# Softmax-attention backward: dK/dV bursts split in odd groups, the turns moved to the fourth unit, turned dQ from group 3 to group 6, and one tile taken from GpSimd

## The chip, the cores and the metric

The kernel runs on one core of one Trainium2 chip. The metric is the time of one execution on the device in microseconds; lower is better. The kernel before has a median of 2526.64 us over 3 runs (2521.6 to 2527.84).

## The reference, cut to what matters

The computation is one block of a transformer (adaptive layer norm, multi-head attention, a squared-ReLU MLP) and its whole backward pass: 2048 positions, model width 512, 32 heads of width 16. The part that the change touches is the backward pass of the attention. The forward part of it in the reference is

```python
    q, k, v = (qkv[0], qkv[1], qkv[2])
    scale = Dh ** (-0.5)
    scores = jnp.einsum('bhqd,bhkd->bhqk', q, k) * scale
    p = _softmax(scores, axis=-1)
    o = jnp.einsum('bhqk,bhkd->bhqd', p, v)
```

and the gradients come from `jax.vjp` of the whole block. For every head the backward pass needs P = exp(scores), dP = dO V^T, dS = P * (dP - row term), and then dV = P^T dO, dK = dS^T Q and dQ = dS K. P is a 2048 x 2048 matrix for each of 32 heads, and it is computed anew.

## The kernel before, in words

The backward attention is written out by hand in `attn_bwd` (L1429 on); its instructions stand on each engine in the order of the code. It takes 32 heads in 16 **pairs** of heads: `g` counts eight quads, `jp` the two pairs of a quad (L1549, L1550). Within a pair, `c` counts four blocks of 512 keys (L1566), and `ib` sixteen tiles of 128 queries, taken in four **groups** of four (L1568, L1575). The text numbers the groups of a pair 0 to 15 (`m` in the code, L1569): groups 0 to 3 are block c = 0, and so on. Each group has four **units**, `i` = 0 to 3; "the fourth unit" is `i == 3`. A unit has two heads, a = 0 and a = 1.

What a unit does, in the order of TensorE (PE):

- For each head, `st` (L1584) computes 128 x 512 scores in a PSUM tile, and ScalarE (ACT) takes the exponential into `pu` (L1587). Right behind each `st` stands `dp` (L1509), which is dP of the unit *before*; VectorE (DVE) multiplies it with that unit's `pu` into `ds` (L1513). `st` and `dp` use opposite halves of the rows of the array. There are three PSUM buffers named "st" and three named "dp". So PE can put an `st` only when ACT has read the one three tiles earlier, and a `dp` only when DVE has read the one three earlier; as PE is in order, whatever stands behind waits too.
- After units 1 and 3, `kv_two` (L1494) adds two earlier units to dK and dV: eight matmuls into `acckv` (L1455), four of which run side by side in four groups of columns. After the last unit of a block, ACT copies `acckv` into `kvT` (L1458); the next block's first `kv` starts `acckv` anew.
- After units 0 and 2, sixteen small matmuls add to dQ in `accq` (L1478). They read `dsT`, the transposed `ds` of a group three groups earlier. The transposition is one DMA per group from the SP queue (L1530). In even groups a part of it, the first 128 x 512 tile, is done by PE and ACT instead (`turn_ds`, L1535: four transposes into an "st" buffer, L1543, and the copy L1544).
- In odd groups (`off`, L1515) one of the eight `ds` tiles, that of `i == 1` and a = 1, is not DVE's: ACT copies `dp` to SBUF (L1521; the buffers are called junk and csq by turns) and GpSimd (POOL) multiplies (L1522).
- The **turns**: dK and dV of the pair before lie transposed in `kvT`. `turn` (L1460) transposes one half of them with eight matmuls into an "st" buffer (L1468), and ACT copies it out with two copies (L1472). dQ is turned by `turn_q` (L1486): DVE scales `accq` into `dqT` (L1483), then four transposes (L1491) and one ACT copy (L1492). The turns wait in the list `turnq`; one is taken at `i == 1` of a group (L1578).

So in every pair but the first, group 1 and group 2 have a dK/dV turn at their second unit, and group 3 the turned dQ, all of the pair before. POOL issues the loads of the next quad, spread over the groups (L1570 to L1573), a small copy (`tick`) ahead of each.

Of the kernel before, what the change touches and what calls it, by code (L numbers as in the profile page):

```python
# [105 lines left out]
class K:  # L106
# [1322 lines left out]
    def attn_bwd(self):  # L1429
# [8 lines left out]
        S, D, H, NQ, ST, SC = self.S, self.D, self.H, self.NQ, self.ST, self.SC  # L1438
        G = 4
# [7 lines left out]
        pend, pendq, turnq = [], [], []  # L1447

        def kv(u):
            (T, g, jp, c, ib, kvT, pu, ds) = u  # L1450
            for j, (n, src) in enumerate((("Q", ds), ("dO", pu))):
                for a in range(2):
                    r = 64 * j + 32 * a
                    col = (2 * jp + a) * DH
                    nc.tensor.matmul(acckv[r:r + DH, :], lhsT=T[n][:, ib, col:col + DH], rhs=src[:, a, :],  # L1455
                                     start=(ib == 0), stop=(ib == ST - 1))
            if ib == ST - 1:
                nc.scalar.activation(kvT[:, 512 * c:512 * (c + 1)], acckv[:], ACT.Copy, scale=kvs[:])  # L1458

        def turn(g, jp, kvT, s0):  # L1460

            if kvT is None:
                return turn_q(g, jp)
            h0 = 4 * g + 2 * jp
            n = ST // 2
            tp = stp.tile([P, n, P], BF16, name="st")
            for st in range(n):
                nc.tensor.transpose(tp[:, st, :], kvT[:, (s0 + st) * P:(s0 + st + 1) * P], self.ident[:])  # L1468
            v = tp[:].rearrange("p s (t a e) -> p t s a e", t=2, a=2)
            for t, dst in enumerate((self.dk_t, self.dv_t)):  # L1470
                d = dst[:, s0:s0 + n, h0 * DH:(h0 + 2) * DH].rearrange("p s (a d) -> p s a d", a=2)
                nc.scalar.copy(d, v[:, t, :, :, 0:DH])  # L1472
# [19 lines left out]
            nc.scalar.copy(self.dq_t[:, :, h0 * DH:(h0 + 2) * DH], tp[:].rearrange("p b (i e) -> p (b i) e", i=G))  # L1492

        def kv_two(n=2):  # L1494
            for u in pend[2 - n:2]:
                kv(u)
            (T, g, jp, c, ib, kvT, pu, ds) = pend[1]
            del pend[:2]
            if c % 2 and ib == ST - 1 and (g, jp) == (NQ - 1, 1):
                turnq.append((g, jp, kvT, 4 * (c - 1)))  # L1500
            elif c == SC - 1 and ib == ST - 1:
                turnq.extend((g, jp, kvT, s0) for s0 in (0, ST // 2))

        def dP(u, a):

            (T, g, jp, c, ib, kvT, pu, dsg, i, grp) = u
            rd = slice(64 - 64 * jp, 128 - 64 * jp)
            dp = dpp.tile([P, 512], F32, name="dp")
            nc.tensor.matmul(dp[:], lhsT=T["dOT"][rd, ib * P:(ib + 1) * P],  # L1509
                             rhs=masked["VT"][a][rd, 512 * c:512 * (c + 1)], start=True, stop=True)  # L1510
            if a == 1 and i == 1 and off(c, ib):
                return dp
            nc.vector.tensor_tensor(dsg[:, i, a], dp[:], pu[:, a, :], ALU.mult)  # L1513

        def off(c, ib):  # L1515
            return (c * SC + ib // G) % 2 == 1

        def dP_pool(u, dp):
            (T, g, jp, c, ib, kvT, pu, dsg, i, grp) = u
            f = (self.junk6, self.csq)[(c * SC + ib // G) // 2 % 2]  # L1520
            nc.scalar.copy(f[:], dp[:])  # L1521
            nc.gpsimd.tensor_tensor(dsg[:, i, 1], f[:], pu[:, 1, :], ALU.mult)  # L1522
# [12 lines left out]
        def turn_ds(dsg, grp, skip):  # L1535

            dsT = dtp.tile([P, 8 * G, P], BF16, name="dsT")
            grp.extend((dsT, 0 if skip else 4))
            if skip:
                return  # L1540
            tp = stp.tile([P, 4, P], BF16, name="st")
            for b in range(4):
                nc.tensor.transpose(tp[:, b, :], dsg[:, 0, 0, b * P:(b + 1) * P], self.ident[:])  # L1543
            nc.scalar.copy(dsT[:, 0:4, :], tp[:])  # L1544

        tick = self.tick
        T = self.T0
        last = None
        for g in range(NQ):  # L1549
            for jp in range(2):  # L1550
                if jp == 0:
                    if g + 1 < NQ:
                        Tn, later = self.load_group(g + 1)
                    else:
                        Tn, later = None, self.wq_pieces(1) + self.load_wmt()
                    cut = len(later) // 2 if Tn else len(later)
                    pieces = self.pair_pieces(g, 1) + later[:cut]
                    later = later[cut:]
                elif g + 1 < NQ:
                    pieces = self.pair_pieces(g + 1, 0) + later  # L1560
                else:
                    pieces = [(self.xhat1_6[:, st, :], self.xhat1_d.rearrange("(st p) d -> p st d", p=P)[:, st, :])
                              for st in range(ST)]
                kvT = kvp.tile([P, S], BF16, name="kvT")
                total = len(pieces)
                for c in range(SC):  # L1566
                    c0 = 512 * c
                    for ib0 in range(0, ST, G):  # L1568
                        m = c * (ST // G) + ib0 // G  # L1569
                        while pieces and (total - len(pieces)) * SC * ST <= m * G * total:  # L1570
                            if last:
                                nc.gpsimd.tensor_copy(tick[:], last[7][0:1, 0, 0, 0:1])
                            nc.gpsimd.dma_start(*pieces.pop(0))  # L1573
                        dsg, grp = self.dsp.tile([P, G, 2, 512], BF16, name="ds"), []
                        for i in range(G):  # L1575
                            ib = ib0 + i
                            q = slice(ib * P, (ib + 1) * P)
                            if turnq and i == 1:  # L1578
                                turn(*turnq.pop(0))
                            pu = self.pup.tile([P, 2, 512], BF16, name="pu")  # L1580
                            for a in range(2):
                                stt = stp.tile([P, 512], F32, name="st")
                                rs = slice(64 * jp, 64 * jp + 64)
                                nc.tensor.matmul(stt[:], lhsT=T["QT"][rs, q], rhs=masked["KT"][a][rs, c0:c0 + 512],  # L1584
                                                 start=True, stop=True)
                                held = dP(last, a) if last else None
                                nc.scalar.activation(pu[:, a, :], stt[:], ACT.Exp, scale=self.scale)  # L1587
                                if held is not None:
                                    dP_pool(last, held)
                            if last:  # L1590
                                dS(last)
                            last = (T, g, jp, c, ib, kvT, pu, dsg, i, grp)
                            if i % 2 == 1 and len(pend) >= 4:
                                kv_two()
                            elif i % 2 == 0 and len(pendq) > 4 * G:
                                for _ in range(8 if len(pendq) > 6 * G else 4):
                                    dq(pendq.pop(0))
                            if i == 2:
                                turn_ds(dsg, grp, off(c, ib))
            T = Tn  # L1600
        with tc.manual_schedule(engines=ALL):
            for t in (2, 0):
                for p in self.wq_pieces(t):
                    nc.gpsimd.dma_start(*p)
            for a in range(2):
                dP(last, a)
            dS(last)
            while len(pend) > 2:
                kv_two()
            kv(pend[0])  # L1610
            for _ in range(2 * G):
                dq(pendq.pop(0))
            kv_two(1)
            k0, v0, k1 = [dpp.tile([P, 512], F32, name="dp") for _ in range(3)]
            self.dw_mm(k0, 1, 0, 0, ST // 2)
            turn(*turnq.pop(0))
            for _ in range(2 * G):
                dq(pendq.pop(0))
            self.dw_mm(v0, 2, 0, 0, ST // 2)
            self.dw_mm(k0, 1, 0, ST // 2, ST)  # L1620
            self.col_sum(1)
            self.dw_mm(v0, 2, 0, ST // 2, ST)
            self.col_sum(2)
            self.cs_bc(1)
            while pendq:
                dq(pendq.pop(0))
            self.cs_bc(2)
            turn(*turnq.pop(0))
            self.dw_mm(k1, 1, 1, 0, ST)
# [312 lines left out]
```

## Time and profile before

| what | value |
|---|---|
| median of 3 runs | 2526.64 us |
| the profiled execution | 2524.31 us, span 2522.4 us |
| mean granted TensorE clock | 0.998 |
| busy over the span | PE 96%, ACT 91%, DVE 68%, POOL 28% |
| backward attention, first `pu` to last | 1169.6 to 2400.5 us of the span |
| a pair without late DMAs | about 76.2 us |

The page gives busy time of each engine and the idle time ahead of each group of instructions. Two cautions for reading it. Instructions overlap: a `pu` takes 0.64 us from start to end, but the next can start 0.48 us after it, so "busy" near 100% does not say that no time is lost; the spacing of starts does. And PE's busy time counts a matmul from its start to its modelled end, and hides waits of some 0.2 us.

### The profile page before, as it was taken

To read this page: it belongs to the slowest core of one execution; us is meant where nothing else is said; L and a number is where in the kernel's file an instruction comes from. 1 tells how busy PE (TensorE), PEld (TensorE's weight loads), DVE (VectorE), ACT (ScalarE), POOL (GpSimd) and SP (SyncE) were. 2 spreads that over 40 slices of the span, in tenths; PEclk is the share of its full clock that TensorE was granted. 3 is DMA by queue.
4 is the path that set the end of the run, shared out by engine and by line. 5 is a ranking of instruction groups with operands and counts; after the bars stand their busy time and mean duration, and the time that the engine had idled before them with its cause. 6 is when DMAs were issued, how large, how long until landed. Compare 5 with 4: busy or idle time off the path is not lost.

```text
span 2522.4 us, 76903 instructions
## 1 busy us (share of the span) xinstructions
PE 2433.1 (96%) x30791; PEld 1107.9 (44%) x30791; DVE 1705.4 (68%) x3519; ACT 2296.2 (91%) x3773; POOL 713.9 (28%) x1289
## 2 busy tenths in 40 slices
PE   8999999999999999989999999999999999999998
PEld 4555555555555554673333333333333333333343
DVE  6222223422332343667999999999999999999957
ACT  7999999999999997535999999999999999999945
POOL 2344531321131022255222222222222222222223
PEclk9999999999999999999999999999999999999999
DMA  4589761441343044699999999999999999999997
GB/s 167 134 178 202 179 114 64 116 99 44 103 118 74 24 137 129 139 191 214 234 221 218 218 226 220 223 227 218 219 218 223 225 221 221 222 228 226 237 211 198
DMA packets 1260558, 446.30 MB, mean 177 GB/s; under 512 B 1204052, under 2 KB 1228246, under 8 KB 1260198
## 3 DMA queue, kind: packets, MB, share of 16 engines
q1 hardware_dynamic: 1219654, 336.29, 70.7%
q0 software_dynamic: 38464, 104.04, 13.9%
q8 instruction: 241, 3.95, 0.7%
q10 hardware_dynamic: 2080, 1.05, 0.1%
q14 instruction: 119, 0.97, 0.1%
HBM read 75.83 MB, written 64.49 MB: 56 GB/s over the span
## 4 chain that ended last, share of the span: by engine, by line
PE 59%; ACT 22%; DMA 11%; issue 4%; DVE 3%; SPq 1%; POOL 0%; DVEq 0%; ACTq 0%; POOLq 0%
ACT pu L391 18%; PE st L1584 17%; DMA dsT<-ds 8%; PE acckv L1455 8%; PE st L388 8%; PE accq L1478 5%; PE accbank L322 3%; PE dp L1509 3%; ACT pu L1587 2%; PE dps L1050 2%; PE pps L1237 2%; PE dps L995 1%; DVE ds L1513 1%; PE st L1543 1%; PE pps L631 1%
## 5 line engine op out<-in xcount | busy, mean ns | idle before, releaser
L1513 DVE TENSOR_TENSOR ds<-dp,pu 128x512 bf16<-128x512 f32 x1920 | 1178.3, 681 | 44.5 <-PE dp L1509 26.4
L1587 ACT ACTIVATE pu<-st 128x512 bf16<-128x512 f32 x2048 | 1073.9, 641 | 39.4 <-PE st L1584 21.3
L391 ACT ACTIVATE pu<-st 128x1024 bf16<-128x1024 f32 x992 | 912.2, 1077 | 5.4 <-PE st L388 5.1
L388 PE MATMUL st<-QTm,KTq 128*128 128x512 bf16 x1984 | 588.4, 377 | 19.7 <-ACT pu L391 6.1
L322 PEld LDWEIGHTS <-pu 128*128 128x128 bf16 x8192 | 347.2, 96 | 236.2 <-issue 3.2
L322 PE MATMUL accbank<-Vaug,pu 128*128 128x17 bf16 x8192 | 357.6, 171 | 1.2 <-ACT Vaug L522 0.9
L1509 PE MATMUL dp<-kvm,q 64*128 64x512 bf16 x1024 | 356.4, 382 | 2.2 <-DVE g2w L1056 0.7
L1509 PE MATMUL dp<-kvm,dOTg 64*128 64x512 bf16 x1024 | 356.2, 382 | 0.9
L1584 PE MATMUL st<-kvm,QTg 64*128 64x512 bf16 x1024 | 327.2, 381 | 10.5 <-ACT pu L1587 7.4
L1584 PE MATMUL st<-kvm,q 64*128 64x512 bf16 x1024 | 326.6, 380 | 10.8 <-ACT pu L1587 7.6
L388 PEld LDWEIGHTS <-KTq 128*128 128x128 bf16 x1984 | 188.2, 96 | 177.5 <-issue 125.9
L1522 POOL TENSOR_TENSOR ds<-junk,pu 128x512 bf16<-128x512 f32 x64 | 73.7, 1151 | 378.6 <-DVE ds L1513 336.7
L1522 POOL TENSOR_TENSOR ds<-csq,pu 128x512 bf16<-128x512 f32 x64 | 73.8, 1154 | 356.6 <-ACT csq L1521 356.6
L302 POOL DMA_DIRECT2D QTm<-QTq_d x124 | 63.5, 514 | 342.7 <-PE st L388 321.3
L1455 PE MATMUL acckv<-ds,Qg 128*16 128x512 bf16 x1024 | 154.3, 381 | 0.0
L1455 PE MATMUL acckv<-pu,dOg 128*16 128x512 bf16 x1024 | 154.2, 381 | 0.0
L1455 PE MATMUL acckv<-pu,q 128*16 128x512 bf16 x1024 | 154.0, 381 | 0.0
L1455 PE MATMUL acckv<-ds,q 128*16 128x512 bf16 x1024 | 154.0, 381 | 0.0
L329 DVE RECIPROCAL rl<-accbank 128x4 f32<-128x4 f32 x128 | 22.9, 179 | 159.5 <-PE accbank L322 159.2
L1584 PEld LDWEIGHTS <-q 64*128 64x128 bf16 x1024 | 58.1, 94 | 137.9 <-issue 104.5
L1584 PEld LDWEIGHTS <-QTg 64*128 64x128 bf16 x1024 | 57.7, 94 | 137.7 <-issue 102.7
L1509 PEld LDWEIGHTS <-q 64*128 64x128 bf16 x1024 | 88.4, 93 | 64.2 <-issue 47.4
(387 smaller groups left out, 3138.6 us busy)
## 6 DMA issues: line engine op xcount, KB each, us to landing
KTq<-KTq_d POOLq DMA_DIRECT2D x24, 512.0 KB, 3.8
duT_d<-auT POOLq DMA_DIRECT2D x3, 1792.0 KB, 8.2
aT_d<-rT POOLq DMA_DIRECT2D x3, 1792.0 KB, 11.6
KTq_d<-KTq SPq DMA_DIRECT2D x32, 128.0 KB, 2.0
QTq_d<-ev_fm SPq DMA_DIRECT2D x32, 128.0 KB, 3.4
ktm_d<-ev_tm POOLq DMA_DIRECT2D x32, 128.0 KB, 2.5
VTq_d<-vT POOLq DMA_DIRECT2D x4, 1024.0 KB, 5.8
dsT<-ds SPq DMA_TRANSPOSE x256, 7.1
```

Of the source, the lines that this page charges most:

```text
L302: nc.gpsimd.dma_start(QTm[j][32 * j:32 * j + 32, :], self.QTq_d[g, 32 * j:32 * j + 32, 512 * qc:512 * (qc + 1)])
L322: nc.tensor.matmul(acc[:, a, sub, :], lhsT=pu[:, a, sub * P:(sub + 1) * P], rhs=Vaug[:, kb, h, :], start=(kb == 0 and a == 0 and sub == 0) ...
L388: nc.tensor.matmul(stt[:, a, :], lhsT=KT[:, kb * P:(kb + 1) * P], rhs=QTm[2 * jp + a][:], start=True, stop=True)
L391: nc.scalar.activation(pu[:], stt[:], ACT.Exp, scale=self.scale)
L1050: nc.tensor.matmul(pt[:], lhsT=a[st], rhs=g_tm[:, st, :], start=(st == 0), stop=(st == ST - 1))
L1455: nc.tensor.matmul(acckv[r:r + DH, :], lhsT=T[n][:, ib, col:col + DH], rhs=src[:, a, :], start=(ib == 0), stop=(ib == ST - 1))
L1478: nc.tensor.matmul(accq[32 * i:32 * i + 32, ib0 // G, :], lhsT=T["K"][:, 4 * c + sub, col:col + 32], rhs=dsT[:, (i * 2 + a) * 4 + sub, :], ...
L1509: nc.tensor.matmul(dp[:], lhsT=T["dOT"][rd, ib * P:(ib + 1) * P], rhs=masked["VT"][a][rd, 512 * c:512 * (c + 1)], start=True, stop=True)
L1513: nc.vector.tensor_tensor(dsg[:, i, a], dp[:], pu[:, a, :], ALU.mult)
L1522: nc.gpsimd.tensor_tensor(dsg[:, i, 1], f[:], pu[:, 1, :], ALU.mult)
L1584: nc.tensor.matmul(stt[:], lhsT=T["QT"][rs, q], rhs=masked["KT"][a][rs, c0:c0 + 512], start=True, stop=True)
L1587: nc.scalar.activation(pu[:, a, :], stt[:], ACT.Exp, scale=self.scale)
```

## The change

Four edits, all in `attn_bwd`.

1. `kv_two(n)` now takes n units from the head of the list. In odd groups it is called with 1, twice: once in the middle of units 1 and 3, between the two heads, and once after them. So the burst of eight matmuls becomes two of four, with an `st` and a `dp` between them. Even groups keep bursts of eight.
2. Turns are taken at `i == 3` and no longer at `i == 1`: in groups 1 and 2 for dK/dV.
3. The turned dQ waits until group 6 (`m >= 6`).
4. In group 1 (`(c, ib // G) == (0, 1)`) the eighth `ds` tile is DVE's too; the copy by ACT and the multiplication by POOL are left out. That is 16 tiles of 128 that POOL had.

```diff
         def kv_two(n=2):
-            for u in pend[2 - n:2]:
+            for _ in range(n):
+                u = pend.pop(0)
                 kv(u)
-            (T, g, jp, c, ib, kvT, pu, ds) = pend[1]
-            del pend[:2]
-            if c % 2 and ib == ST - 1 and (g, jp) == (NQ - 1, 1):
-                turnq.append((g, jp, kvT, 4 * (c - 1)))
-            elif c == SC - 1 and ib == ST - 1:
-                turnq.extend((g, jp, kvT, s0) for s0 in (0, ST // 2))
+                (T, g, jp, c, ib, kvT, pu, ds) = u
+                if ib < ST - 1:
+                    continue
+                if c % 2 and (g, jp) == (NQ - 1, 1):
+                    turnq.append((g, jp, kvT, 4 * (c - 1)))
+                elif c == SC - 1:
+                    turnq.extend((g, jp, kvT, s0) for s0 in (0, ST // 2))
...
-            if a == 1 and i == 1 and off(c, ib):
+            if a == 1 and i == 1 and off(c, ib) and (c, ib // G) != (0, 1):
                 return dp
...
-                            if turnq and i == 1:
+                            if turnq and i == 3 and (turnq[0][2] is not None or m >= 6):
                                 turn(*turnq.pop(0))
...
                                 if held is not None:
                                     dP_pool(last, held)
+                                if a == 0 and i % 2 == 1 and off(c, ib) and len(pend) >= 4:
+                                    kv_two(1)
...
                             if i % 2 == 1 and len(pend) >= 4:
-                                kv_two()
+                                kv_two(1 if off(c, ib) else 2)
...
             while len(pend) > 2:
                 kv_two()
-            kv(pend[0])
+            kv_two(1)
```

The order of PE in an odd group is before `st dp st dp, 16 dQ, st dp st dp, 8 kv`, twice; after, `st dp st dp, 16 dQ, st dp, 4 kv, st dp, 4 kv`, twice. The number of matmuls and of DMAs is the same.

## The prediction

> **What bounds the kernel now.** I read the page's busy shares first, then busy time by stretch, then the timelines of single engines in one pair. The change touches only the backward attention, 1169.6 to 2400.5 us of the span. I take the seventh pair (1630.5 to 1706.7), in which no DMA is late, in its four blocks of four groups:
>
> ```profile
> 1630.73:1651.23 20.50, 20.10 (x294) 7.48 (x296) 19.25 (x32) 20.08 (x43) 4.87 (x11) 1.00 1.03 195
> 1651.23:1669.78 18.55, 18.18 (x268) 6.27 (x263) 18.27 (x31) 18.42 (x38) 4.93 (x11) 1.00 1.14 226
> 1669.78:1688.36 18.58, 18.21 (x268) 6.32 (x271) 18.31 (x31) 18.45 (x38) 4.93 (x11) 1.00 1.19 230
> 1688.36:1706.91 18.55, 18.21 (x263) 6.29 (x263) 18.17 (x30) 18.41 (x38) 5.03 (x11) 1.00 1.16 229
> ```
>
> The columns after the length are busy us of PE, weight loads, DVE, ACT, POOL, then clock, DMA share, GB/s. PE, DVE and ACT are all nearly full, and the first block is 1.95 us longer than the others: it holds the turns. The clock is 1.00, so the throttle plays no part. Where time is lost inside "busy" shows in ACT's and DVE's own timelines of the first block:
>
> ```profile
> 1635.31 0.73 ACT L1458 ACTIVATE kvT<-acckv,kvs 128x512 bf16<-128x512 f32 x1
> 1636.83 0.45 ACT L1472 COPY dk_t<-st 128x256 bf16<-128x256 bf16 x1
> 1639.32 0.69 ACT L1521 COPY junk<-dp 128x512 f32<-128x512 f32 x1
> ...
> 1647.20 0.58 ACT L1492 COPY dq_t<-st 128x512 bf16<-128x512 bf16 x1 [0.26 <-PE st L1491]
> ```
> ```profile
> 1631.42 5.48 DVE L1513 TENSOR_TENSOR ds<-dp,pu 128x512 bf16<-128x512 f32 x9
> 1637.54 4.60 DVE L1513 TENSOR_TENSOR ds<-dp,pu 128x512 bf16<-128x512 f32 x7 [0.63 <-PE dp L1509]
> 1642.40 2.48 DVE L1513 TENSOR_TENSOR ds<-dp,pu 128x512 bf16<-128x512 f32 x4 [0.26 <-PE dp L1509]
> 1644.80 0.68 DVE L1483 TENSOR_SCALAR dqT<-accq 128x512 bf16<-128x512 f32 x1
> ```
>
> From start to start, nine `ds` in 5.48 us less the last one's 0.68 give 0.60 each; a `pu` takes 0.48 (six in 3.07 less 0.64), a 128x512 copy 0.46 (the junk or csq copy), kvT 0.57, a dK/dV copy 0.26, dq_t 0.49. So a block of four groups needs of ACT 32 x 0.48 + 4 x 0.46 + 0.57 = 17.8 us, and of DVE 30 x 0.60 = 18.0. Both are 0.6 to 0.8 under the measured 18.55: two engines with nearly the same load, and PE between them. PE has three "st" and three "dp" buffers, so each waits for the other through PE. In group 5:
>
> ```profile
> 1656.06 0.39 PE L1584 MATMUL st<-kvm,QTg 64*128 64x512 bf16 x1
> 1656.06 0.39 PE L1509 MATMUL dp<-kvm,dOTg 64*128 64x512 bf16 x1
> ...
> 1656.79 0.37 PE L1584 MATMUL st<-kvm,QTg 64*128 64x512 bf16 x1 [0.35 <-ACT pu L1587]
> 1656.80 0.39 PE L1509 MATMUL dp<-kvm,dOTg 64*128 64x512 bf16 x1
> 1657.12 0.39 PE L1455 MATMUL acckv<-ds,Qg 128*16 128x512 bf16 x2
> ...
> 1657.66 0.39 PE L1584 MATMUL st<-kvm,QTg 64*128 64x512 bf16 x1
> ```
>
> The second `st` stands 0.73 behind the first, where 0.22 would do: PE waits for ACT, and only then comes the burst of eight kv, 0.54 us long, ahead of the next `st`. In group 7 the same place waits for DVE instead (second `st` 1665.62, its `dp` 1665.90, burst 1666.20 to 1666.74), and ACT's next `pu` comes 0.30 late. The last thing near its limit is the dsT transposition:
>
> ```profile
> L1530 SPq DMA_TRANSPOSE dsT<-ds  x256: 3419/4113/5953, 1176.1 to 2401.8; - x128
>   PE accq L1478: 13.8, 22
> DMA to landing us min/median/max: 5.3/7.1/10.2
> ```
>
> SP needs 4.1 us to issue one, against groups of 4.4 to 5.3; PE waited 22 times, 13.8 us in all, for one that landed late.
>
> **The change part by part.** Unit: one pair, of which there are 16.
>
> (1) The tile of group 1, the turns, and dQ's departure: groups 0 to 3. ACT loses a copy (0.46) and dq_t (0.49): 32 x 0.48 + 3 x 0.46 + 0.57 + 4 x 0.26 = 18.4 us. DVE gains a tile: (31 + dqT) x 0.60 = 19.2. So DVE becomes this block's limit, and the gain has ends of 0 (ACT's relief goes unused) and 20.50 - 19.2 = 1.3. I take 0.9, walked by hand: without the turn at unit 1, group 1's first `dp` goes out with the `st` at 1635.81, so DVE runs on at 1636.90 and not at 1637.54. From there 22 operations lead to the `ds` of group 3's last unit: 1636.90 + 13.2 = 1650.1, and 0.1 where `dp` comes late behind the moved turn. Before, that `ds` starts at 1651.09. ACT's first `pu` of group 4 comes likewise 0.9 earlier. The turn at unit 3 stalls PE as long (16 dQ 0.34, eight transposes 0.55, in group 2 also turn_ds 0.33), but DVE then has a tile more in hand, and ACT has two `pu` and the dsT copy (1.4 us) to do meanwhile.
>
> (2) dq_t in group 6: 0.49 of ACT and 0.33 of PE, in a block where ACT lost 0.75. Ends 0 and 0.82 (both in a row). Group 7 starts 0.45 later by ACT, of which its 0.30 stall takes up a part: I take +0.3.
>
> (3) The split. Each half of an odd group has two more changes of shape on PE. A change costs 0.10: `st`,`dp` to kv 0.32 against 0.22 of streaming, kv to `st` 0.54 against 2 x 0.22. That is +0.20 a half group, 16 of them per pair, +3.2 us, if PE never waits. But PE does wait there: in group 5 four kv fit between 1656.38 and 1656.70, inside the 0.73; the next `st` pair is out by 1657.10, four kv by 1657.42, and the next `st` comes about 0.25 before 1657.66. In group 7 the first four kv fill 1665.71 to 1666.03 while `dp` waits for DVE until 1665.90; the next `st` comes 0.07 sooner; at unit 3 (`st` 1667.74, `dp` held to 1668.29) 0.11 sooner. DVE's idle before units 2 and 3 (about 0.1 and 0.2 in each odd group) shrinks by these. I take -0.3 for each of the three later blocks (end -0.65, all the loss of DVE and ACT in it); in the first it is in the walk. Losing end: +3.2.
>
> The row above prices a change of shape at 0.10. "TensorEngine Tiling (Array Packing)", Key Properties, in the Trainium skill speaks against the edit: changing the tiling mode drains TensorE. Priced with the about 175 ns of drain in its page "TensorE: Matmul & The Clock Gate", Single matmul latency, an estimate, an odd group of 14 st/dp, kv and dQ streams of 0.22 and 12 changes would need 3.1 + 2.1 = 5.2 us and be PE-bound; by 0.10 it needs 4.3. By the page alone even eight changes would need 4.5, and group 5 takes 4.36: the trace decides for 0.10.
>
> (4) Added wait: in groups 1, 5, 9, 13 the first four kv start `acckv` anew and wait for ACT's kvT copy, with the second `st` and `dp` queued behind, and ACT and DVE behind those. In group 5 the copy ends at 1656.25, the kv could start at 1656.38: 0.13 of room; in group 1 about 0.1. Zero, up to 0.1 each. All kv are the same or earlier, so `pu`, `ds` and loaded tiles come free no later. POOL has 16 x 1.15 us less ahead of its tick copies and loads; it is 28% busy: zero. SP's DMAs are the same; group 1's no longer waits for POOL but for DVE: zero. dqT is rewritten only in the next pair's group 2, dq_t read after the last pair: zero.
>
> (5) Late DMAs: the dQ matmuls come sooner while transpositions land as before. Today's 13.8 us; I add +0.3 a pair, ends 0 and +1.2 (the whole rest).
>
> Sum: (1) + (2) = -0.6 in 15 pairs (the first has no turns, and its first block is already DVE-bound; zero): -9. (3) 16 x 3 x -0.3 = -14.4. (5) 16 x 0.3 = +5. In all -19 on the profiled execution's 2524.3 (span 2522.4 and 1.9 around it), which lies 2.3 under the median: 2505 to 2507. I say **2506**.
>
> **The rivals.** *PE becomes the bound of the odd groups (slower).* For: an odd group would need 4.3 of 4.4 to 4.7 us on PE. Against: the waits of 0.3 to 0.5 ahead of each burst. It decides where PE's wait ahead of the burst is under 0.20; with half the cover gone (3) is +1.6 a pair, +26, less 9, plus 5: 2546; with none 2571. *The split is hidden, only the turns count:* -9: 2515. *Late DMAs take it back:* for, a dsT issue takes 4.1 of 4.6 us and some land just before their dQ; against, nine of the sixteen pairs show under 0.3 us of such waits. At +1.2 a pair the sum is -4: 2520 to 2523, the same. *It does not do what it says:* the program's order shows kv in fours, the turns after unit 2's dQ and dq_t in group 6, so only the size is open.
>
> **How the numbers follow.** Forecast 0.60 (own range 2488 to 2513), turns alone 0.10, DMAs 0.11, PE-bound 0.19. A measurement tells 0.3%, 7.6 us, from no change: faster 0.70, same 0.11, slower 0.19. The low end, 2486, is the forecast with (3) at its full 0.65 and (5) at +0.3 (-35) and (1) at 1.1; the high end, 2538, takes in the DMA case and the milder half of the PE case.
>
> **What would show it.** Right: groups 0 to 3 of a pair near 19.6 us, 4 to 7 near 18.5, the others near 18.3; kv rows in halves with an `st` between; DVE idle before `ds` in a pair down from 2.2 to about 1. Wrong: odd groups at 4.6 or more with kv, `st` and `dp` back to back, ACT idle behind them (PE-bound); or accq waiting for dsT for 30 us and more (DMAs). The forecast fails most easily at (3), whose gain is a tenth here and there.

## The result, and the profile after

The changed kernel takes as long as the one before: 2522.63 us (median of 14 runs, 2517.38 to 2527.45) against 2522.3 us (14 runs, 2517.95 to 2531.45), a ratio of 0.9998 with a 95% interval of 0.9988 to 1.0008. The forecast was 2506. A second set of runs later, `after_2` below, gave 0.9999.

The two profiled executions alone would tell another story. That of the changed kernel took 2517.38 us (span 2515.6), the fastest of its 14; that of the kernel before took 2524.31, above its median. Their difference of 7 us is in no median. So what follows takes pairs without late DMAs for the inner working, and whole times for verdicts.

The pages agree with a change that did what it says: busy PE 97%, ACT 91%, DVE 68%, POOL 28%, clock 0.997. Here is the twelfth pair of the changed kernel, in which no DMA is late, by stretches of four groups. As before, the columns after the length are busy us of PE, weight loads, DVE, ACT and POOL, then clock, DMA share, GB/s.

```profile
2007.93:2027.63 19.70, 19.65 (x283) 7.32 (x281) 19.54 (x33) 19.46 (x42) 3.82 (x10) 1.00 1.18 202
2027.63:2046.62 18.99, 18.60 (x270) 6.99 (x268) 18.70 (x32) 18.94 (x40) 5.07 (x11) 1.00 1.16 236
2046.62:2065.00 18.38, 18.22 (x266) 6.71 (x264) 18.31 (x31) 18.33 (x38) 5.02 (x11) 1.00 1.09 219
2065.00:2083.41 18.41, 18.30 (x265) 6.79 (x264) 18.35 (x31) 18.36 (x38) 5.03 (x11) 1.00 1.18 233
```

The first block came down from 20.50 to 19.70, where 19.6 was forecast. The second went up from 18.55 to 18.99, where 18.5 was forecast; the last two came down by 0.2 and 0.14, where 0.3 was forecast. The pair is 0.7 us shorter, not 1.5.

DVE's own timeline of the first block shows the first step as it was walked:

```profile
2007.34 14.28 DVE L1515 TENSOR_TENSOR ds<-dp,pu 128x512 bf16<-128x512 f32 x23
2021.54 0.68 DVE L1483 TENSOR_SCALAR dqT<-accq 128x512 bf16<-128x512 f32 x1
2022.13 18.49 DVE L1515 TENSOR_TENSOR ds<-dp,pu 128x512 bf16<-128x512 f32 x30
```

Fifty-three `ds` and one dqT stand in a row, without the waits of 0.63 and 0.26 us that were there before. In the whole pair DVE now idles 0.6 us ahead of its `ds`, against 2.2; the prediction expected about 1. Of the 1.6 us won, the one extra `ds` a pair, 0.60, takes back more than a third. This view joins rows over short waits, though: thirty `ds` make (18.49 - 0.68) / 29 = 0.614 from start to start, where nine in a row gave 0.60 before. One by one most steps are 0.60 still, and the rest lies in a few longer ones, shown further below.

PE in group 5, two half-bursts (not shown) between three `st`, in the place of one burst:

```profile
2032.69 0.39 PE L1586 MATMUL st<-kvm,QTg 64*128 64x512 bf16 x1
...
2033.42 0.37 PE L1586 MATMUL st<-kvm,QTg 64*128 64x512 bf16 x1
...
2034.07 0.39 PE L1586 MATMUL st<-kvm,QTg 64*128 64x512 bf16 x1
```

The second `st` still stands 0.73 behind the first, so the first four kv are indeed hidden in that wait. The third stands 1.38 behind the first, against 1.60 before: 0.22 sooner, where 0.25 was forecast. But DVE's steps around this burst are 0.60 both before and after, so there the sooner `st` has no idle time to take away.

The idle time of an odd group stands around units 2 and 3. Here are PE at unit 3 of the same group, then DVE's `ds` of that stretch, and last the first and the last `ds` of the same stretch in the kernel before (group 7 of its seventh pair).

```profile
2035.09 0.39 PE L1511 MATMUL dp<-kvm,dOTg 64*128 64x512 bf16 x1
2035.40 0.39 PE L1455 MATMUL acckv<-ds,Qg 128*16 128x512 bf16 x2
...
2035.73 0.39 PE L1511 MATMUL dp<-kvm,dOTg 64*128 64x512 bf16 x1
```
```profile
2034.90 0.68 DVE L1515 TENSOR_TENSOR ds<-dp,pu 128x512 bf16<-128x512 f32 x1
2035.61 0.69 DVE L1515 TENSOR_TENSOR ds<-dp,pu 128x512 bf16<-128x512 f32 x1
2036.26 0.69 DVE L1515 TENSOR_TENSOR ds<-dp,pu 128x512 bf16<-128x512 f32 x1
...
2037.51 0.68 DVE L1515 TENSOR_TENSOR ds<-dp,pu 128x512 bf16<-128x512 f32 x1
```
```profile
1667.56 0.68 DVE L1513 TENSOR_TENSOR ds<-dp,pu 128x512 bf16<-128x512 f32 x1
...
1670.27 0.68 DVE L1513 TENSOR_TENSOR ds<-dp,pu 128x512 bf16<-128x512 f32 x1
```

A change of shape costs 0.10 here again: `dp` to kv takes 0.31 and kv to the next `dp` 0.33, against 0.22 of streaming. So the `dp` come 0.64 to 0.65 apart, and DVE, which has caught up, follows at PE's pace: its steps are 0.71, 0.65, 0.64 and 0.61, and those `ds` start 0.52 behind their `dp`, where the other tiles start 0.62 to 1.06 behind (medians over the last two blocks of pairs 2 to 15). Before, the four steps were 0.70, 0.61, 0.79 and 0.61. The stretch is down from 2.71 to 2.61, and two odd groups a block make 0.2.

ACT in group 6, where the turned dQ now leaves:

```profile
2040.09 0.62 ACT L1546 COPY dsT<-st 128x512 bf16<-128x512 bf16 x1
2040.56 0.65 ACT L1492 COPY dq_t<-st 128x512 bf16<-128x512 bf16 x1
2041.03 4.26 ACT L1589 ACTIVATE pu<-st 128x512 bf16<-128x512 f32 x8
```

Two copies of 0.47 each, back to back, stand between two `pu`. From `pu` to `pu` group 6 takes 4.99 us in this kernel and took 4.46 before (medians of pairs 2 to 15): the copy adds about its whole length.

Last, the transposition of `ds`, by its line of code; the three figures after the count are the ns that one takes on SP (shortest, median, longest).

```profile
L1532 SPq DMA_TRANSPOSE dsT<-ds x256: 3412/4201/5957, 1174.8 to 2392.8; - x128
  PE accq L1478: 17.5, 29
```

PE waited 29 times for one that was late, 17.5 us in all, against 22 times and 13.8 us before. In the profile of `after_2`, of the same kernel, it was 35 times and 23.5 us: this row varies from one execution to the next and is read with the times beside it.

### The profile page after: what moved, and what is told of

The parts are those of the page before. It is cut to its first block, busy times and chain, and to the rows that moved or that the text cites. A ratio compares the mean times of both kernels' runs of the same rounds, so it can differ in the third digit from the quotient of the medians.

```text
span 2515.6 us, 76906 instructions
## 1 busy us (share of the span) xinstructions
PE 2438.2 (97%) x30791; PEld 1131.3 (45%) x30791; DVE 1720.2 (68%) x3535; ACT 2293.5 (91%) x3757; POOL 698.6 (28%) x1273
## 4 chain that ended last, share of the span: by engine, by line
PE 56%; ACT 24%; DMA 13%; issue 4%; DVE 2%; POOL 1%; SPq 0%; DVEq 0%; ACTq 0%; POOLq 0%
ACT pu L391 18%; PE st L1586 15%; DMA dsT<-ds 10%; PE st L388 8%; PE acckv L1455 8%; PE accq L1478 5%; ACT pu L1589 4%; PE accbank L322 3%; PE dps L1050 2%; PE pps L1237 2%; PE dp L1511 2%; PE dp L1639 2%; PE st L1545 1%; PE pps L631 1%; PE st L1734 1%
## 5 line engine op out<-in xcount | busy, mean ns | idle before, releaser
L1515 DVE TENSOR_TENSOR ds<-dp,pu 128x512 bf16<-128x512 f32 x1936 | 1190.8, 684 | 22.5 <-PE dp L1511 13.3
L1586 PE MATMUL st<-kvm,QTg 64*128 64x512 bf16 x1024 | 347.1, 381 | 4.7
L1586 PE MATMUL st<-kvm,q 64*128 64x512 bf16 x1024 | 346.4, 381 | 4.3
L1455 PE MATMUL acckv<-ds,Qg 128*16 128x512 bf16 x1024 | 176.0, 382 | 0.0
L1455 PE MATMUL acckv<-pu,dOg 128*16 128x512 bf16 x1024 | 176.0, 382 | 0.0
L1455 PE MATMUL acckv<-ds,q 128*16 128x512 bf16 x1024 | 175.8, 382 | 0.0
L1455 PE MATMUL acckv<-pu,q 128*16 128x512 bf16 x1024 | 175.8, 382 | 0.0
L1524 POOL TENSOR_TENSOR ds<-junk,pu 128x512 bf16<-128x512 f32 x48 | 55.4, 1155 | 275.5 <-DVE ds L1515 163.1
L1586 PEld LDWEIGHTS <-q 64*128 64x128 bf16 x1024 | 67.4, 93 | 141.7 <-issue 109.7
L1478 PE MATMUL accq<-dsT,Kg 128*32 128x128 bf16 x4096 | 104.9, 221 | 11.2 <-DMA dsT<-ds 10.9
```

What stands on the lines that cost most here:

```text
L1478: nc.tensor.matmul(accq[32 * i:32 * i + 32, ib0 // G, :], lhsT=T["K"][:, 4 * c + sub, col:col + 32], rhs=dsT[:, (i * 2 + a) * 4 + sub, :], ...
```

## The experiments

All ratios are to the kernel before on the same chip, with a 95% interval. Theories are told in words here; where an expectation uses letters, A is the theory that late transpositions take the gain back, and E that edit 4 moves a load of GpSimd to where it delays them.

### First round: which part, and is it the wait for dsT?

The theory was that the compute side gained what was forecast, or most of it, and that the wait of dQ for late transpositions took it back. The rival: the split is worth nothing, or costs, and the wait is noise. The first two runs do parts of the change alone; the other two take the wait away, by giving each transposition half a group more time.

**`split_only`**: edit 1 alone.

```diff
-            if a == 1 and i == 1 and off(c, ib) and (c, ib // G) != (0, 1):
+            if a == 1 and i == 1 and off(c, ib):
...
-                            if turnq and i == 3 and (turnq[0][2] is not None or m >= 6):
+                            if turnq and i == 1:
```

> Only the first edit: the kv bursts split in odd groups; turns, dQ's turn and GpSimd's tile as before. Theory A (the split pays a little in every block, late DMAs take most of it back): the later three blocks of a pair without late DMAs at 18.4 us against 18.57 before, the first near 20.2 against 20.50, the shortest pair near 75.4 against 76.16; the whole 0 to 6 us faster than before, because the dQ matmuls wait more for transposed ds. Rival B (the split's extra changes of shape on TensorE cost what it hides, all gain in the first block comes from the turns): blocks at 18.57 and 20.5, the whole unchanged and no more DMA waits.

Measured: 2520.85 us against 2525.23, ratio 0.9984 (0.9967 to 1.0001). The shortest pair is 75.78 us, in blocks of 20.57, 18.39, 18.41 and 18.39, against 76.16 and 20.50, 18.52, 18.57, 18.57 before. So the split wins 0.13 to 0.18 in each of the three later blocks, half of the forecast 0.3, and nothing in the first. In the whole time the interval takes in 1, so a gain there is not shown by this run alone.

**`no_split`**: edits 2, 3 and 4 without the split.

```diff
-                                if a == 0 and i % 2 == 1 and off(c, ib) and len(pend) >= 4:
-                                    kv_two(1)
...
-                                kv_two(1 if off(c, ib) else 2)
+                                kv_two()
```

> Edits two to four without the first: turns in the fourth unit, turned dQ in group 6, group 1's tile on VectorE, kv bursts of eight everywhere. Theory A: first block 19.8 to 20.0 us (20.50 before, 19.63 to 19.75 with all edits), second block 19.1 to 19.2 because the turned dQ costs 0.5 to 0.6 there, the other two 18.57 as before; the shortest pair about 76.0, the whole within 3 us of before. Rival B: first block 19.65 as with all edits, shortest pair near 75.7, 5 to 8 us faster less DMA waits.

Measured: 2529.64 us against 2525.23, ratio 1.0015 (1.0003 to 1.0028). Its shortest pair is 75.94 us (19.84, 18.93, 18.58, 18.58), 0.22 shorter than before. A pair that is shorter when no DMA is late, in a kernel that is 4 us longer: the loss lies outside such pairs. In whole times the parts add up by the medians: the split is worth about -4 us, edits 2 to 4 about +4, and together 0.

**`after_half`**: the whole change, with the dQ matmuls half a group later.

```diff
-                            elif i % 2 == 0 and len(pendq) > 4 * G:
-                                for _ in range(8 if len(pendq) > 6 * G else 4):
+                            elif i % 2 == 0 and len(pendq) > 5 * G:
+                                for _ in range(8 if len(pendq) > 7 * G else 4):
```

> All four edits, and the dQ matmuls of a group come half a group (about 2.3 us) later than in the changed kernel, so that the transposed ds may land later; four transposed tiles are still enough. Theory A (late DMAs take back what the edits gain): waits of the dQ matmuls for transposed ds fall from 14.9 us in the groups (profile of the changed kernel) to under 4, all pairs come near the shortest, 75.5, and the whole is 8 to 14 us faster than before. Rival C (the gain is lost elsewhere, at the tail behind the last pair or in variation between executions): DMA waits fall, but the whole stays within 4 us of before.

Measured: 2534.53 us against 2525.23, ratio 1.0036 (1.0022 to 1.0049): slower, not faster.

**`before_half`**: the kernel before with the same delay, and so with the turned dQ in group 4.

```diff
-                            if turnq and i == 1:
+                            if turnq and i == 1 and (turnq[0][2] is not None or m >= 4):
...
-                            elif i % 2 == 0 and len(pendq) > 4 * G:
-                                for _ in range(8 if len(pendq) > 6 * G else 4):
+                            elif i % 2 == 0 and len(pendq) > 5 * G:
+                                for _ in range(8 if len(pendq) > 7 * G else 4):
```

> None of the four edits, only the dQ matmuls half a group later (and so the turned dQ in group 4 instead of 3). Theory A: DMA waits fall from 14.2 us in the groups to under 4, the pairs stand at 76.2, and the whole is 4 to 10 us faster than before; the changed kernel with the same delay is 6 to 10 us faster than this one, which is the edits' own gain when no DMA is late. Rival C: within 3 us of before, and no gap of more than 4 us to the changed kernel with the same delay.

Measured: 2530.36 us against 2525.23, ratio 1.0024 (1.0011 to 1.0037).

Both runs miss, and the lines of `after_half` on the transposition say a part of why:

```profile
L1532 SPq DMA_TRANSPOSE dsT<-ds x256: 3454/4260/8213, 1173.0 to 2403.5; - x128
  DVE ds L1515: 10.3, 14
  PE accq L1478: 1.0, 1
```

The wait of PE is gone (1.0 us, once), as planned. But now DVE waits, 10.3 us in 14 places (6.7 us in 10 in `before_half`): a `ds` buffer is free for the group three later only when its transposition has read it. A consumer that comes later gives a slow producer no more room when the producer also holds the buffers of the engine ahead of it. Part of the loss is there without late DMAs too: the shortest pair is 75.71 against 75.43, and 76.44 against 76.16 for the kernel before, 0.28 us by 16 pairs or 4.5 us. What follows: putting dQ later does not remove the cost of late transpositions; whether their own length is what counts, the next runs ask.

### Second round: how much the transpositions take, and which edit makes them take more

**`before_light`**: the kernel before with 16 blocks of 128 x 128 in each transposition (there are 28 or 32), which are read twice in the place of all; the other blocks are left out of dQ.

```diff
-                                 rhs=dsT[:, (i * 2 + a) * 4 + sub, :],
+                                 rhs=dsT[:, 16 + ((i * 2 + a) * 4 + sub) % 16, :],
...
-                nc.sync.dma_start_transpose(dsT[:, n:, :], dsg[:].rearrange("p i a k -> p (i a k)")[:, n * P:])
+                nc.sync.dma_start_transpose(dsT[:, 16:, :], dsg[:].rearrange("p i a k -> p (i a k)")[:, 16 * P:])
```

> The kernel before with the transposition DMA of each group cut to its last 16 blocks of 128 x 128 (of 32, or 28 in even groups); the dQ matmuls are as many as ever, but read those 16 blocks twice, so dQ is left out of the result and only its time is kept. Theory A (the transpositions are nearly a fourth limit, and their lateness hides the edits' gain): dQ waits fall from 14 us to under 2, every pair stands at 76.2 us, and the whole is 8 to 14 us faster than before. Rival C (gain lost elsewhere): under 4 us.

**`after_light`**: the changed kernel with the same two lines.

> All four edits, with the transposition DMA cut in the same way (dQ not right, its time kept). Theory A: every pair at 75.4 to 75.5 us, and 9 to 13 us faster than the kernel before cut in the same way: the gain that the edits have where no DMA is late. Rival C: pairs at 75.4, but the whole within 4 us of the cut kernel before, the rest lost at the tail. Rival D (pairs were short only by luck of that execution): pairs near 76.

Measured: `before_light` 2510.19 us against 2526.43, ratio 0.9936 (0.9918 to 0.9955); `after_light` 2499.5, ratio 0.9891 (0.987 to 0.9911). Here is the whole stage, from the first `pu` to the last, in the windows view of the kernel before, the changed kernel, `before_light` and `after_light`:

```profile
1169.60:2400.50 1230.90, 1192.17 (x17095) 416.98 (x17095) 1186.24 (x1937) 1207.58 (x2444) 316.60 (x632) 1.00 1.17 222
```
```profile
1168.30:2389.90 1221.60, 1195.52 (x17095) 439.61 (x17095) 1198.90 (x1953) 1204.72 (x2428) 299.95 (x616) 1.00 1.20 223
```
```profile
1166.50:2385.20 1218.70, 1193.18 (x17095) 416.39 (x17095) 1185.27 (x1937) 1204.75 (x2444) 316.59 (x632) 1.00 0.65 129
```
```profile
1169.30:2377.00 1207.70, 1196.68 (x17095) 439.91 (x17095) 1196.87 (x1953) 1200.78 (x2428) 299.04 (x616) 1.00 0.66 130
```

With the DMA share down from 1.17 and 1.20 to 0.65, the change wins 11.0 us of the stage (1218.70 to 1207.70), and 10.7 us of the time (2510.19 to 2499.5). That is what it is worth on the engines, against 23.4 forecast for steps (1) to (3). And in `after_light` the line of the transposition no longer has PE's dQ among those who wait:

```profile
L1532 SPq DMA_TRANSPOSE dsT<-ds x256: 1569/1641/3632, 1175.8 to 2378.2; - x128
```

The other difference is what the full transpositions cost each kernel. For the one before it is 1 - 0.9936 = 0.64%, or 16 us; for the changed one 0.9998 - 0.9891 = 1.07%, or 27 us. The change makes them 11 us dearer, with some 7 us of uncertainty by the three intervals, and so gives back what it wins. This 11 is a remainder, the change's whole effect (none) less its gain in the light kernels; it was not counted from waits.

**`no_tile`**: edits 1, 2 and 3; the eighth tile of group 1 stays with GpSimd.

```diff
-            if a == 1 and i == 1 and off(c, ib) and (c, ib // G) != (0, 1):
+            if a == 1 and i == 1 and off(c, ib):
```

> Edits one to three; group 1's tile stays with ScalarE and GpSimd. Theory A: ScalarE has a copy of 0.46 us more in the first block, VectorE 0.60 less; the first block 19.9 to 20.2 us against 19.63 to 19.75, the others 18.9, 18.4, 18.4; shortest pair near 75.8, the whole 0 to 4 us slower than with all edits, so 0 to +4 us against before. If the tile is what makes DMAs late, the whole is instead 3 to 6 us faster than before.

Measured: 2515.33 us against 2526.43, ratio 0.9962 (0.9948 to 0.9976): faster than both kernels. Its shortest pair is 75.47 us (19.69, 18.98, 18.39, 18.39), nearly that of the changed kernel (75.43). So edit 4 wins 0.06 us in the first block, not the tile's 0.46 of ACT, and costs about 9 us somewhere else.

**`dq3`**: the changed kernel with the turned dQ in group 3 again.

```diff
-                            if turnq and i == 3 and (turnq[0][2] is not None or m >= 6):
+                            if turnq and i == 3 and (turnq[0][2] is not None or m >= 3):
```

> All edits but the third: the turned dQ goes out in group 3, at its fourth unit. Theory A: the turned dQ costs its 0.5 to 0.6 us wherever it stands: first block 20.2, second 18.4 (19.63 and 18.87 with all edits), shortest pair 75.3 to 75.6, the whole within 3 us of the changed kernel. The prediction's step that priced dQ in group 6 at 0.3 would instead have this one 3 to 5 us slower than the changed kernel.

Measured: 2526.41 us against 2526.43, ratio 1.0005 (0.9994 to 1.0016). The shortest pair is 75.47 us, in blocks of 20.11, 18.40, 18.43 and 18.39. The turned dQ costs the same 0.5 us where it stands first (20.11 against 19.63) as in group 6 (18.87 to 18.98 against 18.40). Edit 3 moves a cost from one block to another and wins nothing that shows.

### Third round: what edit 4 does to the DMAs

Edit 4 takes 1.15 us of multiplication off GpSimd, 16 times, and GpSimd also issues loads. The prediction wrote that down as free. With the tile gone, the load of the next pair's `kvm` that stood behind it goes out at once; these are lines of GpSimd's timeline, of the changed kernel in its twelfth pair (first `pu` at 2007.93), and, further below, of the kernel without edit 4 in its eighth (first `pu` at 1700.18):

```profile
2015.49 0.51 POOL L1575 DMA_DIRECT2D kvm<-VTq_d  x1 [0.32 <-PE dp L1511]
```

The load goes out 7.6 us into the pair. So the theory for this round: the 72 KB load now falls beside the transpositions of groups 0 and 1 and makes them late. The rivals: DVE's extra tile makes `ds`, and so the transposition, later; or the tile's time on ACT and DVE shifts the groups against the DMAs in some other way.

**`after_2`**: the changed kernel again, beside the other three.

> The changed kernel once more, beside the next two on the same chip. If the tile of group 1 makes DMAs late (theory E), it stands at 0.999 to 1.001 of before, 5 us or more behind the kernel that leaves the tile with GpSimd. If the gap between those two in the earlier run was only one of chips (rival G), all three of this call stand within 3 us.

Measured: 2521.55 us against 2521.94, ratio 0.9999 (0.9987 to 1.0012).

**`no_tile_2`**: `no_tile` again.

> Edits one to three, the tile of group 1 left with ScalarE and GpSimd. Theory E: 0.996 of before again, 7 to 10 us faster than before and than the changed kernel. Rival G: within 3 us of the changed kernel.

Measured: 2514.94 us against 2521.94, ratio 0.9971 (0.996 to 0.9982). The gain over both kernels stands, in two rounds on two chips.

```profile
1709.09 1.15 POOL L1524 TENSOR_TENSOR ds<-junk,pu 128x512 bf16<-128x512 f32 x1 [5.67 <-ACT junk L1523]
...
1710.31 0.56 POOL L1575 DMA_DIRECT2D kvm<-VTq_d  x1
```

With GpSimd's tile ahead of it, the same load goes out 10.1 us into the pair.

**`tile_hold`**: the whole change, and GpSimd multiplies two tiles of `pu` with each other in that place, into a buffer that nobody reads, so that the load is held up while DVE keeps the tile.

```diff
+                                elif a == 1 and last and last[8] == 1 and (last[3], last[4] // G) == (0, 1):
+                                    nc.gpsimd.tensor_tensor(self.junk6[:], last[6][:, 1, :], last[6][:, 0, :], ALU.mult)
```

> All four edits, and GpSimd does a multiplication of the same size in group 1 whose result nobody reads, at the place of the one that went; so its later tick copies and loads come as late as without edit 4. Theory E in its first form (without that work GpSimd issues the next loads some 2 us sooner, where they meet other transpositions): 5 to 9 us faster than the changed kernel, level with the kernel that leaves the tile. Second form (it is VectorE's extra tile itself, not GpSimd's timing): level with the changed kernel. Rival G: no difference anywhere.

Measured: 2518.28 us against 2521.94, ratio 0.9991 (0.998 to 1.0003). The load went out 8.7 us into the pair, later than the 7.5 of the changed kernel but not at 10.1, since the stand-in needs no copy by ACT and starts sooner.

**`no_tile_light`**: `no_tile` with the 16-block transposition.

> Edits one to three with the transposition DMA cut to 16 blocks (dQ not right, its time kept). If the tile is worth nothing to the engines, pairs at 75.4 to 75.6 us and the whole within 2 us of the changed kernel cut in the same way (0.989 of before), so that any gap between the full kernels comes from late DMAs alone. If the tile itself costs VectorE time that the shortest pairs do not show, 3 to 8 us faster than that.

Measured: 2496.97 us against 2521.94, ratio 0.9902 (0.9883 to 0.9921); its stage is 1207.5 us, that of `after_light` 1207.8, and the ratios of the two, 0.9902 and 0.9891, differ by less than their intervals. With light transpositions edit 4 makes no difference that shows, so what it costs hangs on the DMAs. For this kernel the full transpositions cost 0.9971 - 0.9902 = 0.69% by this round, 0.60% with the ratio of `no_tile`: 15 to 17 us, about what they cost the kernel before, each with some 5 us of uncertainty.

**`no_tile_early`**: edits 1 to 3, with GpSimd's tile, and the load alone moved ahead of it.

```diff
+                            if m == 1 and i == 2 and pieces:
+                                nc.gpsimd.tensor_copy(tick[:], last[7][0:1, 0, 0, 0:1])
+                                nc.gpsimd.dma_start(*pieces.pop(0))
                             pu = self.pup.tile([P, 2, 512], BF16, name="pu")
```

> Edits one to three, group 1's tile with GpSimd; only the load that GpSimd issues for group 2 is put ahead of that tile, into group 1, so that it goes out about 8 us after a pair's first exponential and not 10.4, as edit 4 makes it. Theory E (edit 4 costs time by the place of this load alone): transpositions of groups 0 and 1 go from 4.2 and 4.4 us to 4.5 and 4.7, and the whole is 5 us or more slower than with the load in its place: 0.999 to 1.001 of before. Second form (VectorE's extra tile is what makes them late): 0.996 to 0.998, as without the move.

Measured: 2522.63 us against 2525.14, ratio 0.9988 (0.9973 to 1.0003). The order came out as meant, the load ahead of the tile and again 7.5 us into the pair (the tile's multiplication starts at 1709.08):

```profile
1707.69 0.51 POOL L1584 DMA_DIRECT2D kvm<-VTq_d  x1 [0.32 <-PE dp L1511]
```

The table puts the runs side by side: when the load goes out in most pairs, and how long SP needs for the transposition of groups 0 and 1, worked out from the trace as the mean over the second to the fifteenth pair.

| kernel | GpSimd has the tile | load out, us into the pair | group 0, us | group 1, us | ratio to before |
|---|---|---|---|---|---|
| before | yes | 10.8 | 4.26 | 4.38 | 1 |
| `split_only` | yes | 10.7 | 4.02 | 4.38 | 0.9984 |
| `no_tile` | yes | 10.1 | 4.14 | 4.33 | 0.9962 |
| `no_tile_2` | yes | 10.1 | 4.19 | 4.46 | 0.9971 |
| `tile_hold` | no | 8.7 | 4.08 | 4.40 | 0.9991 |
| `no_tile_early` | yes | 7.5 | 4.52 | 4.72 | 0.9988 |
| `no_split` | no | 7.6 | 4.27 | 4.63 | 1.0015 |
| `dq3` | no | 7.5 | 4.55 | 4.57 | 1.0005 |
| changed | no | 7.5 | 4.41 | 4.65 | 0.9998 |
| `after_2` | no | 7.5 | 4.59 | 4.71 | 0.9999 |

Where the load goes out at 7.5, group 0 takes 4.27 to 4.59 and group 1 4.57 to 4.72; where it goes out later, 4.02 to 4.26 and 4.33 to 4.46, about 0.3 less in each by the means, whoever has the tile. That part of the theory is shown, by means that scatter by 0.1 to 0.2 each: `no_tile_early` differs from `no_tile` in the load's place alone. Over all sixteen groups of a pair the means run from 67.1 to 69.8 us, each uncertain by 0.6 to 1.0, and do not part the kernels. In time, `no_tile_early` is 4 to 7 us behind `no_tile` by the ratios (0.9988 against 0.9971 and 0.9962), some half or more of the 7 to 9 us between `no_tile` and the change, though the intervals overlap by a little. And `tile_hold` has short transpositions in these two groups and is still at 0.9991. Its interval touches those of all the others, so it neither proves nor excludes a share for DVE's extra tile. That share stays open: no run holds the load to the old time with edit 4 kept.

Nor do the profiles show where edit 4's 7 to 9 us are lost. PE's waits for late transpositions are 18.3 and 16.9 us in `no_tile` and `no_tile_2`, and 17.5 and 23.5 in the two profiles of the changed kernel. The first block, on average over pairs 2 to 15, stands 0.12 and 0.15 above the shortest of its profile without edit 4 and 0.30 and 0.33 with it, which makes 2 to 3 us.

## Why the prediction was wrong

The forecast was faster by 19 us, and the case that came true was the third rival, that late DMAs take it back (chance 0.11, 2520 to 2523). Its number came true, but not its account, for it left the gain of 23 us whole and let the DMAs take nearly all of it. Two things failed: the gain of steps (1) to (3) was put twice too high, by (2) and (3), and the DMAs' answer in (4) and (5) at half of what it was. By the runs, a pair without late DMAs went like this:

| step | predicted, us a pair | measured, us a pair | from |
|---|---|---|---|
| (1) first block | -0.9 | -0.87 | 20.50 to 19.63, shortest blocks |
| (2) dq_t in group 6 | +0.3 | +0.5 to +0.6 | 18.98 against 18.39 in `no_tile`; 20.11 against 19.63 in `dq3` |
| (3) split, three blocks | -0.9 | -0.47 | 18.52, 18.57, 18.57 to 18.39, 18.41, 18.39 in `split_only` |
| (1) to (3), all pairs, us | -23.4 | -10.7 | 2510.19 to 2499.5, the two light kernels |
| (5) late DMAs, all pairs, us | +5 | +11 | 16 and 27 us; a remainder, some 7 either way |
| sum, us | -19 | 0 | 2522.3 to 2522.63 |

**Step (1)** was right, to 0.03 us, and its walk shows in DVE's timeline. Only its account of the parts was wrong: it added the tile of edit 4 as a relief of ACT. Without it the block is 19.69, and without the split 19.84, so the turns' new place and dq_t's leaving do most of it, and the split 0.2.

**Step (2)** said that group 7's stall of 0.30 would take up a part of the copy. Step (3) let the split use up that same stall. Idle time was counted twice. Without the split (`no_split`) dq_t makes group 6 longer by 0.48 (4.46 to 4.94) and group 7 shorter by 0.11 (4.63 to 4.52), and costs the block 0.41 (18.93 against 18.52). With the split group 7 is 4.57, as it is in `split_only` without dq_t there (4.56): nothing is taken up, and the block pays 0.5 to 0.6.

**Step (3)** had its mechanism half right. The first four kv do hide in PE's wait, a change of shape does cost 0.10, and in group 5 the next `st` comes 0.22 sooner where 0.25 was said. The term that failed is "-0.3 for each of the three later blocks": it let DVE's idle time before units 2 and 3, about 0.1 and 0.2 in each odd group, shrink by what each `st` gains. The steps before unit 2 stayed as long as they were (0.71), and of the other 0.2 a half went: 0.10 an odd group, 0.13 to 0.18 a block in the runs. The bursts of unit 1, with their 0.25 and 0.07, fell where DVE did not wait. What is left is set by PE. Its `dp` come 0.65 apart there, of which 0.20 are the two changes of shape, against DVE's 0.60; there PE has no wait any more in which they could hide.

On the price of a change of shape the Trainium skill's page "TensorEngine Tiling (Array Packing)", Key Properties, warns that switching the mode drains TensorE. It does show, at 0.10 us a change, in both kernels; it was hidden at unit 1, where PE waited anyway, and not at unit 3. So the rival that made PE the bound of the odd groups came true for three tiles of each, and no further: odd groups did not grow (4.36 and 4.63 us before, 4.30 and 4.57 after).

**Step (4)** at zero is consistent with all runs: the last two blocks lost nothing. But within it stands a sentence that failed: "POOL has 16 x 1.15 us less ahead of its tick copies and loads; it is 28% busy: zero." It asked whether GpSimd had time, and not what its loads would meet when they went out 3 us sooner. Leaving that one edit out makes the kernel 7 to 9 us faster (`no_tile`, twice), and with light transpositions it costs nothing that shows.

**Step (5)** was mis-sized, +5 for +11, and put down to the wrong event. It made dQ sooner against transpositions "as before". In the runs the transpositions themselves became slower, in groups 0 and 1 by about 0.3 us, and giving dQ more time made the kernel slower (`after_half`, `before_half`). By the ratios nearly all of the 11 hangs on edit 4: without it the transpositions cost 15 to 17 us, against 16 before the change. The load's place is shown to lengthen the transpositions, and by the medians, whose intervals overlap, it carries half of the cost or more; the rest is open.

Of the two faults the first weighs more. With (1) to (3) at their true -10.7 and (5) at its +5 the sum is -6, already within the 0.3%; with (5) at +11 and the rest as forecast it is -12, still faster.

## What to carry to other kernels

Idle time that two edits want to use is there only once: subtract it from the trace after the first edit, before the second is priced, and look at which tiles it stands. An operation that comes sooner where nobody waits wins nothing. Where a DMA stream fills most of its period (here 4.2 us of a group of 4.6), a step taken off an issuing engine is no free gift: look at which load goes out sooner, and what is on the DMA engines then. A kernel with its DMA stream thinned, run for the version before and after, parts what a change wins on the engines from what it costs in transfers, which no single profile did here.

The version that beats both kernels is edits 1 to 3 without edit 4: 2515.33 and 2514.94 us, ratios 0.9962 (0.9948 to 0.9976) and 0.9971 (0.996 to 0.9982).

## What the runs showed of the hardware

- A 72 KB load from GpSimd's queue that goes out about 3 us sooner lengthens the issue of the two neighbouring transpositions on SP by about 0.3 us each, of 4.1 to 4.4. The two queues do not run apart: "DMA: Bandwidth & Descriptors" in the Trainium skill, Issuing engines are not separate DMA queues, says that DMAs run on the same 16 DMA engines and interleave, whichever engine started them, and the table of the third round is in keeping with it.
- The transposition acts as a fourth limit of the stage. With it in full the stage moves 222 GB/s with a DMA share of 1.17, and the kernel takes 16 us longer than with 16 of its 28 or 32 blocks, at 129 GB/s and 0.65. In that kernel neither PE nor DVE shows a wait for it, and SP issues one in 1.64 us against 4.1 to 4.2: less than a half of the time for a half of the blocks or a little more.
- A change between the shape of `st` and `dp` and that of the kv matmuls costs PE 0.10 us. Where PE puts `st`, `dp` and four kv again and again, a pass takes 0.65 us, and DVE, which could take a tile each 0.60, follows at 0.65.
- Later reading of a transposed buffer did not help where the source buffers are freed by the transposition: PE's 17.5 us of waits became 1.0 and 10.3 us of DVE's, and the kernel 0.4% slower than the change without the delay.
